# Attention on one Trainium2 core: V products of three or two key tiles right behind their scores, and PSUM banks named by hand

## The chip, the cores and the metric

The kernel runs on one core of one Trainium2 chip. The metric is device time in microseconds of one execution; lower is better. The time before is the median of three runs.

## The reference, cut to what matters

The reference is one transformer-like block on 2048 tokens of width 448, in float32. A modulation vector made from `c` scales and shifts two layer norms and gates two branches. The first branch is attention with 16 heads of width 28, the second a gated MLP whose gate mixes over the tokens. The change lies in attention:

```python
qkv = (x @ wqkv).reshape(B, S, 3, H, Dh).transpose(2, 0, 3, 1, 4)
q, k, v = qkv[0], qkv[1], qkv[2]
scores = jnp.einsum("bhqd,bhkd->bhqk", q, k) * (Dh ** -0.5)
p = softmax(scores, axis=-1)
o = jnp.einsum("bhqk,bhkd->bhqd", p, v)
attention = o.transpose(0, 2, 1, 3).reshape(B, S, D) @ wo
...
x = x + ga * attention
```

## The kernel before

The order of the work is written out by hand: each engine executes its instructions in the order in which the Python program issues them, and waits on semaphores where a buffer is not ready. Five engines take part: TensorE (PE) multiplies into PSUM banks, VectorE (DVE) and ScalarE (ACT) read PSUM, GpSimd (POOL) works in the on-chip memory only, and SyncE (SP) issues most transfers. PSUM has eight banks here; seven form the pool `ring`, from which `bank(name)` takes the next tile of 128 x 512 floats, and one is the pool `ps_o`, which holds a head's output sum `o_ps`. Which of the seven banks a tile of `ring` gets is decided by the pool while the program is built, and a tile's first matmul waits until the last reader of its bank is done.

After the norm of the input and the projections (`qk_unit`: a matrix of 128 x 512 in 11 matmuls into a bank `pq`, then two copies `qf` and `qh` by ScalarE and a subtraction by POOL), attention goes through 256 units `u`: 16 heads of 16 key tiles. For a unit

- `s_mm(u, qb)` multiplies one key tile of 128 keys with a quarter of the queries (512) into a bank `st_ps` (L603), and ScalarE takes the exponential into a tile `P` of the on-chip memory (L607). There are four quarters.
- `m_mm(j, kb)` makes, for the head that comes next, the scores of 128 queries with 512 keys into a bank `mt` (L572), and VectorE reduces them to a maximum per query (L577). This is needed since the exponential subtracts a maximum, which the transposed scores of `s_mm` carry as extra rows of the operand. `j` is 20 units ahead (`LEAD`).
- `pv_mm(u)` multiplies V with the four quarters of `P` and adds into `o_ps` (L618). V has 32 columns (28, and ones for the sum), so the four quarters use four column strips of 32 of the array. The profile shows two matmul records for each of these float32 matmuls, eight a unit.

The main loop before, for each unit `u`: four scores and four maximum scores in turn, then, on every even unit, the V products of units `u - 2` and `u - 1`. So TensorE changes 118 times into the V products and back in units 0 to 235. After these there is no next head, and the last 20 units have scores and V products only.

Around the units stand steps that are set to a slot, in two lists, `events` (issued before the unit's scores) and `late` (issued after its V products). At a head's end, `n_copy` has ScalarE copy `o_ps` out (L626), and `n_sum`, `n_recip`, `n_bcast`, `n_mul` and `n_scatter` divide it by its sum and store it by way of transfers, VectorE and POOL. Four units before a head, `m_max` reduces the maxima per query (L583, VectorE) and `m_fin` transposes them on TensorE (a bank `mtp`, L588), copies them twice on ScalarE (`nf`, `nh`), subtracts on POOL (`nl`), and stores two rows into the query operand by SP. Beside them run transfers and sums for a later stage (`ws_load`, `ws_add`, `ws_store`: SP and POOL).

Before unit 0 comes a ramp: 18 projection units with the first 81 maximum scores between their matmuls (`m_first`), from 86 to 152 us of the span.

Of the kernel before, what the change touches and what calls it, by code (L numbers as in the profile page):

```python
# [8 lines left out]
F32 = mybir.dt.float32  # L9
# [4 lines left out]
PSUM = bass.MemoryType.PSUM  # L14
DRAM = bass.MemoryType.DRAM

S, D, H, DH, FH = 2048, 448, 16, 28, 896
EPS = 1e-5
SCALE = DH ** -0.5
NT = S // 128  # L20
# [13 lines left out]
def tile_adaln_mha_gmlp(ctx, tc, x, wqkv, wo, w_in, w_spT, b_sp, w_out, cT, w_mod, out):  # L34
# [36 lines left out]
    class Halves:  # L71


        def __init__(self, n, lo, hi):
            self.n, self.views = n, (lo, hi)
# [34 lines left out]
    def ln_transpose(xns, full_pool, dsts, scol, bcol, engs, los=(pool,) * 4, mid=None, after=None):  # L110

        tps = []
        for c in range(4):
            tp = bank("tp")
            tps.append(tp)
            for t in range(4):
                pe.transpose(tp[:, t * 128 : (t + 1) * 128], xns[t][:, c * 128 : (c + 1) * 128], ident)  # L117
        if mid:
            mid()
        for c in (0, 2, 1, 3):  # L120
            tp = tps[c]
            f = full_pool.tile([128, 512], F32, name="hfull")
            if engs[c] is act:
                act.activation(f, tp, AF.Identity, scale=scol[:, c : c + 1], bias=bcol[:, c : c + 1])
            else:
                engs[c].tensor_scalar(
                    out=f, in0=tp, scalar1=scol[:, c : c + 1], scalar2=bcol[:, c : c + 1], op0=ALU.mult, op1=ALU.add
                )
            hi = dsts[:, c if c < 3 else 6, :]
            if engs[c] is act:  # L130
                act.activation(hi, f, AF.Copy)
            else:
                engs[c].tensor_copy(hi, f)
            if c < 3:
                sub(los[c], dsts[:, 3 + c, :], f, hi)
            else:
                sub(los[c], hi[64:128], f[64:128], hi[64:128])
            if after:
                after(c)


    ps = ctx.enter_context(ExitStack())
    ring = ps.enter_context(tc.tile_pool(name="ring", bufs=7, space=PSUM))
    ps_o = ps.enter_context(tc.tile_pool(name="ps_o", bufs=1, space=PSUM))

    att = ctx.enter_context(ExitStack())
    vpool = att.enter_context(tc.tile_pool(name="vpool", bufs=1))
# [13 lines left out]
    dve.memset(ones_r.bitcast(F32), 1.0)  # L161
    wms, xts, raws = {}, {}, {}

    def bank(name):
        return ring.tile([128, 512], F32, name=name, tag="s")

    def load_mod(pair, eng):
        for k in range(4):
# [48 lines left out]
    dve.tensor_tensor(out=silu, in0=cc_t, in1=ec, op=ALU.mult)  # L217

    pcs = {c: bank("pc") for c in (0, 2)}
    wu = bank("wu")  # L220

    def pe_fill(n, with_):
# [272 lines left out]
    for g in range(1, NG):  # L495
        if g == 3:
# [16 lines left out]
            def load_head(h, c0=0, c1=S):  # L513
                k, q = kst[h % 3], qst[h % 3]
                if h > 2:
                    sp.dma_start(q[84:86, :].bitcast(F32), q[86:88, :].bitcast(F32))
                for r0, i in ((0, 0), (56, 1), (28, 0)):
                    sp.dma_start(k[r0 : r0 + 28, c0:c1].bitcast(F32), qk_scr[i][D + h * DH : D + (h + 1) * DH, c0:c1])
                for r0, i in ((0, 0), (28, 1), (56, 0)):
                    sp.dma_start(q[r0 : r0 + 28, c0:c1].bitcast(F32), qk_scr[i][h * DH : (h + 1) * DH, c0:c1])  # L520
# [48 lines left out]
    def m_mm(j, kb):  # L569
        h, t = divmod(j, NT)  # L570
        mt = bank("mt")
        pe.matmul(  # L572
            mt, qst[h % 3][:, t * 128 : (t + 1) * 128], kst[h % 3][:, kb * 512 : (kb + 1) * 512], start=True, stop=True
        )
        if h not in pms:
            pms[h] = npool.tile([128, NT, 4], F32, name="pm")
        dve.tensor_reduce(out=pms[h][:, t, kb : kb + 1], in_=mt, axis=AX.X, op=ALU.max)  # L577
# [22 lines left out]
    def s_mm(u, qb):  # L600
        h, kt = divmod(u, NT)
        st = bank("st_ps")
        pe.matmul(st, kst[h % 3][:, kt * 128 : (kt + 1) * 128], qst[h % 3][:, qb * 512 : (qb + 1) * 512], start=True, stop=True)  # L603
        if qb % 2 == 0:
            ptiles[u, -1] = ppool.tile([128, 2, 512], F32, name="P")
        p = ptiles[u, -1][:, qb % 2, :]
        act.activation(p, st, AF.Exp, scale=SCALE)  # L607
        ptiles[u, qb] = p
# [4 lines left out]
    def pv_mm(u):  # L613
        h, kt = divmod(u, NT)
        if kt == 0:
            otile[h] = ps_o.tile([128, 512], F32, name="o_ps", tag="o")
        for qb in range(4):
            pe.matmul(  # L618
                otile[h][32 * qb : 32 * qb + 32, :], V[:, kt, h, :], ptiles.pop((u, qb)), start=kt == 0, stop=kt == NT - 1
            )  # L620
# [109 lines left out]
    LEAD = 20  # L730
    NU = H * NT
    events, late = {}, {}

    def at(slot, fn, *a, when=events):
        when.setdefault(slot, []).append((fn, a))

    for h in range(H):
        if h >= 2:
            at(h * NT - LEAD - 10, load_head, h)
        e0 = (h + 1) * NT  # L740
        at(e0 + 1, n_copy, h)
        at(e0 + 2, n_sum, h)
        at(e0 + 4, n_recip, h)
        at(e0 + 6, n_bcast, h)
        at(e0 + 8, n_mul, h)
        at(e0 + 9, n_scatter, h)
        at(h * NT + NT - LEAD, m_max, h)
        at(max(h * NT + NT - LEAD, -2), m_fin, h, when=late)
    for c, hl in ((0, 4), (1, 9), (2, 13)):
        for qb in range(4):  # L750
# [5 lines left out]
    for i in range(4):  # L756
        at(120 + 8 * i, wo_load, i)
        at(124 + 8 * i, wo_prep, i)
        at(200 + 8 * i, win_first, i)

    load_head(1)

# [15 lines left out]
    for i, (m, g) in enumerate(units):  # L778
        qk_unit((m,), g, {j: m_first for j in ((1, 3, 5, 7, 9) if i < 8 else (1, 4, 7, 10))})

    for u in range(NU + 1):
        for fn, a in events.pop(u, []):
            fn(*a)
        j = u + LEAD
        for qb in range(4 if u < NU else 0):
            s_mm(u, qb)
            if j < NU:
                m_mm(j, qb)
        if u % 2 == 0 and u > 0:
            pv_mm(u - 2)  # L790
            pv_mm(u - 1)
        for fn, a in late.pop(u, []):
            fn(*a)
    tail_events = {fn.__name__: [(fn, a)] for k in sorted(events) for fn, a in events[k]}

    def run_tail(*names):
        for nm in names:
            for fn, a in tail_events.pop(nm):
                fn(*a)

    run_tail("n_copy")


    att.close()
# [104 lines left out]
    h = H - 1  # L909
# [465 lines left out]
```

## Time and profile before

| | before |
|---|---|
| median of 3 runs | 1408.03 us (1407.81 to 1408.63) |
| profiled execution | 1407.25 us, its span 1405.5 us |
| granted TensorE clock | 1.0 |
| units 0 to 235 in the trace | 151.6 to 831.6 us |
| TensorE busy | 1393.3 us |
| VectorE busy | 1014.1 us |
| ScalarE busy | 788.9 us |

The profile shows for each group of instructions the engine, the tile written and the tiles read, the number, the busy time and the mean duration, and the idle time of the engine just before, with what ended it. Matmuls are pipelined, so one begins well before the last one's record ends: read their starts, not their durations. PEld are the weight loads, which overlap the matmuls; a load carries the wait for the bank of its matmul. Waits and chains are inferred from semaphore events.

### The profile page before, as it was taken

The page shows a single profiled execution, that of the slowest core. Times are in us where ns is not written, and L with a number is a line of the kernel's source. Part 1 is how long each engine was busy: PE and PEld are TensorE (multiplying, and loading weights), DVE is VectorE, ACT ScalarE, POOL GpSimd, SP SyncE. Part 2 cuts the span into 40 slices and gives each one's busy share as a digit, 9 for nine tenths or more (in the row PEclk, how much of TensorE's full clock was granted, in tenths as well). Part 3 has the DMA queues.
Part 4 walks back from the last instruction along what each step waited for, and adds up shares of the span by engine and source line. Part 5 has one row for each costly group of instructions (what it writes and reads, how often), then busy time and mean ns, then how long its engine had stood idle before and what let it go on. Part 6 is the DMA issues. An engine that isn't in the chain of part 4 may idle for free.

```text
span 1405.5 us, 20321 instructions
## 1 busy us (share of the span) xinstructions
PE 1393.3 (99%) x7164; PEld 981.2 (70%) x7164; DVE 1014.1 (72%) x1701; ACT 788.9 (56%) x1536; POOL 296.3 (21%) x284
## 2 busy tenths in 40 slices
PE   7999999999999999999999999999999999999999
PEld 7887655555555555555555554988998888888888
DVE  7798888888888888888888860751356655668574
ACT  4723677777777777777677779263234544434211
POOL 4234313122314243313200021100143430001000
PEclk9999999999999999999999999999999999999999
DMA  8564645555455556654422001534103333444453
GB/s 256 156 169 168 187 110 171 167 161 157 154 167 171 150 164 179 178 158 150 123 68 75 21 18 45 187 115 139 53 0 113 107 113 111 142 140 157 142 174 108
DMA packets 99377, 187.01 MB, mean 133 GB/s; under 512 B 17736, under 2 KB 29130, under 8 KB 96730
## 3 DMA queue, kind: packets, MB, share of 16 engines
q1 hardware_dynamic: 96846, 181.88, 43.0%
q10 hardware_dynamic: 2430, 3.84, 0.7%
q8 instruction: 56, 0.92, 0.3%
q14 instruction: 45, 0.37, 0.1%
HBM read 130.42 MB, written 50.46 MB: 129 GB/s over the span
## 4 chain that ended last, share of the span: by engine, by line
PE 96%; DMA 2%; DVE 1%; ACT 0%; issue 0%; SPq 0%; POOL 0%; DVEq 0%; ACTq 0%; POOLq 0%
PE st_ps L603 19%; PE o_ps L618 17%; PE mt L572 17%; PE acc L1143 6%; PE acc L1142 6%; PE acc L1144 6%; PE z_ps L1068 5%; PE z_ps L954 5%; PE pq L318 5%; PE wo_ps L824 3%; PE pv L300 2%; PE y_ps L1247 2%; PE y_ps L1248 2%; PE y_ps L1246 2%; PE tp L117 1%; DMA wm<-in_w_mod_dram 1%
## 5 line engine op out<-in xcount | busy, mean ns | idle before, releaser
L577 DVE TENSOR_REDUCE pm<-mt 128x1 f32<-128x512 f32 x1024 | 631.5, 682 | 110.0 <-PE mt L572 109.8
L607 ACT ACTIVATE P<-st_ps 128x512 f32<-128x512 f32 x1024 | 513.2, 621 | 150.0 <-PE st_ps L603 150.0
L603 PE MATMUL st_ps<-qst,kst 128*128 128x512 f32 x1024 | 407.5, 409 | 0.1
L572 PE MATMUL mt<-kst,qst 128*128 128x512 f32 x1024 | 402.1, 393 | 0.6 <-DVE pm L577 0.3
L603 PEld LDWEIGHTS st_ps<-qst,kst 128*128 128x128 f32 x1024 | 191.1, 187 | 151.4 <-issue 82.2
L618 PE MATMUL o_ps<-P,V 128*32 128x512 f32 x2048 | 247.5, 598 | 0.0
L572 PEld LDWEIGHTS mt<-kst,qst 128*128 128x128 f32 x1024 | 192.5, 188 | 32.9 <-DVE pm L577 2.3
L725 POOL TENSOR_TENSOR ws_raw<-ws_raw 128x512 f32<-128x512 f32 x80 | 102.9, 1287 | 282.8 <-DMA ws_raw<-in_w_spT_dram 270.4
L1030 ACT ACTIVATE wsp_h<-raw_sp 128x512 fp32r<-128x512 f32 x112 | 69.9, 631 | 154.4 <-PE acc L1144 103.6
L84 DVE TENSOR_TENSOR wsp_l<-raw_sp,wsp_h 128x512 fp32r<-128x512 f32 x112 | 82.0, 743 | 81.9 <-ACT wsp_h L1030 81.2
L618 PEld LDWEIGHTS o_ps<-P,V 128*32 128x32 f32 x2048 | 54.1, 109 | 123.5 <-issue 116.6
L1143 PE MATMUL acc<-wsp_l,heapA 128*128 128x512 f32 x224 | 87.4, 390 | 0.3 <-DVE wsp_l L84 0.2
L1142 PE MATMUL acc<-wsp_h,heapA 128*128 128x512 f32 x224 | 87.3, 390 | 0.0
L1144 PE MATMUL acc<-wsp_h,heapA 128*128 128x512 f32 x224 | 87.2, 389 | 0.0
L1143 PE MATMUL acc<-wsp_l,heapB 128*128 128x512 f32 x174 | 67.7, 389 | 0.0
L1144 PE MATMUL acc<-wsp_h,heapB 128*128 128x512 f32 x174 | 67.7, 389 | 0.0
L1142 PE MATMUL acc<-wsp_h,heapB 128*128 128x512 f32 x174 | 67.7, 389 | 0.0
L318 PE MATMUL pq<-heapD,heapD 128*128 128x512 f32 x196 | 61.9, 390 | 0.0
L1072 DVE BATCH_NORM_STATS2 stz<-z 128x6 f32<-128x448 f32 x32 | 19.9, 625 | 50.4 <-ACT z L1071 30.1
L1143 PEld LDWEIGHTS acc<-wsp_l,heapA 128*128 128x128 f32 x224 | 42.0, 188 | 9.6 <-DVE wsp_l L84 1.2
L1142 PEld LDWEIGHTS acc<-wsp_h,heapA 128*128 128x128 f32 x224 | 42.0, 188 | 9.0 <-DVE cD L1148 0.3
L1144 PEld LDWEIGHTS acc<-wsp_h,heapA 128*128 128x128 f32 x224 | 42.0, 188 | 8.8
(212 smaller groups left out, 1605.7 us busy)
## 6 DMA issues: line engine op xcount, KB each, us to landing
ws_raw<-in_w_spT_dram SPq DMA_DIRECT2D x160, 256.0 KB
ws_scr<-ws_raw SPq DMA_DIRECT2D x80, 256.0 KB
raw_sp<-ws_scr SPq DMA_DIRECT2D x80, 256.0 KB
kst<-qk_scr SPq DMA_DIRECT2D x45, 224.0 KB
qst<-qk_scr SPq DMA_DIRECT2D x45, 224.0 KB
raw_sp<-in_w_spT_dram SPq DMA_DIRECT2D x32, 256.0 KB
qk_scr<-qh SPq DMA_DIRECT2D x28, 256.0 KB
qk_scr<-ql SPq DMA_DIRECT2D x28, 256.0 KB
```

Of the source, the lines that this page charges most:

```text
L84: eng.tensor_tensor(out=dst, in0=a, in1=hi.bitcast(F32), op=ALU.subtract)
L318: pe.matmul(pq, wqk[:, b, m * 128 : (m + 1) * 128], hT[g][:, a, :], start=j == 0, stop=j == NST - 1)
L572: pe.matmul(mt, qst[h % 3][:, t * 128 : (t + 1) * 128], kst[h % 3][:, kb * 512 : (kb + 1) * 512], start=True, stop=True)
L577: dve.tensor_reduce(out=pms[h][:, t, kb : kb + 1], in_=mt, axis=AX.X, op=ALU.max)
L603: pe.matmul(st, kst[h % 3][:, kt * 128 : (kt + 1) * 128], qst[h % 3][:, qb * 512 : (qb + 1) * 512], start=True, stop=True)
L607: act.activation(p, st, AF.Exp, scale=SCALE)
L618: pe.matmul(otile[h][32 * qb : 32 * qb + 32, :], V[:, kt, h, :], ptiles.pop((u, qb)), start=kt == 0, stop=kt == NT - 1)
L725: pool.tensor_tensor(out=a, in0=a, in1=b, op=SUMS[i // 16][2])
L954: pe.matmul(ps_t, w1[:, b, f * 128 : (f + 1) * 128], h2T[g][:, a, :], start=j == 0, stop=j == NST - 1)
L1142: pe.matmul(acc[i], zh, hi, start=st == 0, stop=False)
L1143: pe.matmul(acc[i], zh, lo, start=False, stop=False)
L1144: pe.matmul(acc[i], zl, hi, start=False, stop=st == 7)
```

## The change

The order of units 0 to 235 becomes rounds of 3, 3, 3, 3, 2 and 2 key tiles for each head. A round issues all scores of its tiles with as many maximum scores between them, and then the V products of the same tiles, which before belonged to an earlier pair. The last 20 units keep their form. `n_copy` moves one unit earlier (before the first scores of the next head, since its V products now end with the head), and `m_max` moves from before a unit's scores to behind the V products, beside `m_fin`; both come after the round that holds the last maximum score of their head.

The seven banks are named in the program and no longer given out by the pool. In the ramp (`Ramp`) two banks go to the projections in turn and five to all else. In the units (`First`) a small count follows TensorE, VectorE and ScalarE in steps of a matmul, and gives each tile the bank that it holds to come free first. For this the pool `ring` is closed before the ramp, a second pool with seven named tiles stands in its place, and this one is closed again behind attention. `ps_o` is allocated before them.

```diff
     ps = ctx.enter_context(ExitStack())
-    ring = ps.enter_context(tc.tile_pool(name="ring", bufs=7, space=PSUM))
     ps_o = ps.enter_context(tc.tile_pool(name="ps_o", bufs=1, space=PSUM))
+    ring_s = ExitStack()
+    ring = [ring_s.enter_context(tc.tile_pool(name="ring", bufs=7, space=PSUM))]
...
+    chooser = [None]
+
     def bank(name):
-        return ring.tile([128, 512], F32, name=name, tag="s")
+        if chooser[0] is None:
+            return ring[0].tile([128, 512], F32, name=name, tag="s")
+        return ring[0].tile([128, 512], F32, name=name, tag=f"b{chooser[0](name)}", bufs=1)
...
-        at(e0 + 1, n_copy, h)
+        at(e0 if e0 < NU - LEAD else e0 + 1, n_copy, h)
...
-        at(h * NT + NT - LEAD, m_max, h)
+        at(h * NT + NT - LEAD, m_max, h, when=late if h else events)
...
+    class Ramp:
+        def __init__(self):
+            self.n = [0, 0]
+
+        def __call__(self, name):
+            k = int(name != "pq")
+            self.n[k] += 1
+            return 2 + self.n[1] % 5 if k else self.n[0] % 2
+
+    class First:
+        def __init__(self):
+            self.t, self.eng, self.free = 0.0, {}, [0.0] * 7
+
+        def __call__(self, name):
+            b = min(range(7), key=self.free.__getitem__)
+            self.t = max(self.t + 1, self.free[b] + 0.3)
+            a = max(self.eng.get(name, 0.0), self.t + 1.9)
+            self.eng[name] = a + (2.1 if name == "st_ps" else 2.6)
+            self.free[b] = a + (2.6 if name == "st_ps" else 3.0)
+            return b
+
+        def pause(self, n):
+            self.t += 3.75 * n + 1.5
+
+    ring_s.close()
+    ring[0] = ring_s.enter_context(tc.tile_pool(name="ring2", bufs=1, space=PSUM))
+    chooser[0] = Ramp()
+
     load_head(1)
...
-    for u in range(NU + 1):
-        for fn, a in events.pop(u, []):
+    chooser[0] = First()
+
+    def run_at(u, when):
+        for fn, a in when.pop(u, []):
             fn(*a)
-        j = u + LEAD
+
+    u = 0
+    for n in [n for _ in range(H) for n in (3, 3, 3, 3, 2, 2)]:
+        if u == NU - LEAD:
+            break
+        for k in range(u, u + n):
+            run_at(k, events)
+            for qb in range(4):
+                s_mm(k, qb)
+                m_mm(k + LEAD, qb)
+        for k in range(u, u + n):
+            pv_mm(k)
+        chooser[0].pause(n)
+        u += n
+        for k in range(u - n + 1, u + 1):
+            run_at(k, late)
+    for u in range(NU - LEAD, NU + 1):
+        run_at(u, events)
         for qb in range(4 if u < NU else 0):
             s_mm(u, qb)
-            if j < NU:
-                m_mm(j, qb)
-        if u % 2 == 0 and u > 0:
+        if u % 2 == 0 and u > NU - LEAD:
             pv_mm(u - 2)
             pv_mm(u - 1)
-        for fn, a in late.pop(u, []):
-            fn(*a)
+            chooser[0].pause(2)
+        run_at(u, late)
...
     run_tail("n_copy")
+    ring_s.close()
+    ring[0] = ps.enter_context(tc.tile_pool(name="ring", bufs=7, space=PSUM))
+    chooser[0] = None
```

## The prediction, made before the changed kernel ran

> **What bounds the kernel now.** I read the page first: the busy shares, the chain that ended last and the costliest groups.
>
> ```profile
> PE 1393.3 (99%) x7164; PEld 981.2 (70%) x7164; DVE 1014.1 (72%) x1701; ACT 788.9 (56%) x1536; POOL 296.3 (21%) x284
> ...
> PE st_ps L603 19%; PE o_ps L618 17%; PE mt L572 17%; PE acc L1143 6%; PE acc L1142 6%; PE acc L1144 6%; PE z_ps L1068 5%; PE z_ps L954 5%; PE pq L318 5%; PE wo_ps L824 3%; PE pv L300 2%; PE y_ps L1247 2%; PE y_ps L1248 2%; PE y_ps L1246 2%; PE tp L117 1%; DMA wm<-in_w_mod_dram 1%
> ...
> L577 DVE TENSOR_REDUCE pm<-mt 128x1 f32<-128x512 f32 x1024 | 631.5, 682 | 110.0 <-PE mt L572 109.8
> L607 ACT ACTIVATE P<-st_ps 128x512 f32<-128x512 f32 x1024 | 513.2, 621 | 150.0 <-PE st_ps L603 150.0
> ```
>
> Attention's three matmul lines (scores L603, maximum scores L572, V products L618) are 53% of the chain, all of it TensorE. VectorE's maxima and ScalarE's exponentials empty the banks and show idle time that ends on TensorE: the engine that sets the end is TensorE, for now. The next question is how much room the other two leave, which is seen inside one round. The timeline of one pair of key tiles, eight scores, eight maximum scores and then the V products of an earlier pair:
>
> ```profile
> 500.65 0.19 PEld L603 LDWEIGHTS st_ps<-qst,kst 128*128 128x128 f32 x1 [0.84 <-issue]
> 500.65 0.50 PE L603 MATMUL st_ps<-qst,kst 128*128 128x512 f32 x1
> 500.99 0.40 PE L572 MATMUL mt<-kst,qst 128*128 128x512 f32 x1
> ...
> 501.19 4.03 ACT L607 ACTIVATE P<-st_ps 128x512 f32<-128x512 f32 x8 [1.69 <-PE st_ps L603]
> 501.42 4.88 DVE L577 TENSOR_REDUCE pm<-mt 128x1 f32<-128x512 f32 x8 [0.85 <-PE mt L572]
> ...
> 504.20 0.39 PE L572 MATMUL mt<-kst,qst 128*128 128x512 f32 x1
> 504.52 0.16 PEld L618 LDWEIGHTS o_ps<-P,V 128*32 128x32 f32 x8 [0.36 <-issue]
> 504.98 0.13 PEld L618 LDWEIGHTS o_ps<-P,V 128*32 128x32 f32 x4 [0.30 <-issue]
> 505.41 0.13 PEld L618 LDWEIGHTS o_ps<-P,V 128*32 128x32 f32 x4 [0.30 <-issue]
> 506.38 0.50 PE L603 MATMUL st_ps<-qst,kst 128*128 128x512 f32 x1
> ```
>
> From start to start: the round takes 506.38 - 500.65 = 5.73 us. An ordinary matmul step is (504.20 - 500.99) / 14 = 0.229 us. The first step is 0.34 (its weights are loaded in the open: 0.11 more), the step into the V products 0.32, and these take 506.38 - 504.52 = 1.86 in four sets, 0.43 from set to set and more at the first and the last. Two sets are one key tile's products.
>
> ScalarE needs 4.03 us for eight exponentials; with the group's 0.62 for one, they end (4.03 - 0.62) / 7 = 0.487 apart. VectorE needs 4.88 for eight maxima, with 0.68 for one: 0.60 apart. A score and a maximum score together take TensorE only 0.459. So inside the burst of scores both readers fall behind, and they catch up during the V products. That is the fact on which the forecast rests.
>
> **The long stretch: fewer changes of kind.** The change does 60 rounds of three tiles and 28 of two over units 0 to 235, where there were 118 rounds of two. In the built kernels' instruction order every matmul is there as before; only the places differ. A round of three is a round of two plus eight steps and two sets: 5.73 + 8 x 0.229 + 2 x 0.43 = 8.42. So 118 x 5.73 = 676.1 becomes 60 x 8.42 + 28 x 5.73 = 665.6: **-10.5 us** if nothing waits. The stretch itself is known:
>
> ```profile
> 151.60:831.60 680.00, 679.92 (x3775) 387.35 (x3774) 579.23 (x971) 488.13 (x987) 156.25 (x140) 1.00 0.48 138
> ```
>
> 680.0 against 676.1: all transposes and waits of today are 3.9 us, most of them at the transposes, which stay. I take 0.7 of them as gone.
>
> **The long stretch: the banks run out in a round of three.** Seven banks hold scores and maximum scores. When may a matmul follow a reader? A wait in the present kernel shows it:
>
> ```profile
> 242.92 3.67 DVE L577 TENSOR_REDUCE pm<-mt 128x1 f32<-128x512 f32 x6
> 244.04 0.40 PE L572 MATMUL mt<-kst,qst 128*128 128x512 f32 x1
> 244.25 0.19 PEld L603 LDWEIGHTS st_ps<-qst,kst 128*128 128x128 f32 x1 [0.26 <-DVE pm L577]
> 244.60 0.40 PE L572 MATMUL mt<-kst,qst 128*128 128x512 f32 x1
> ```
>
> The second of these maxima ends at 242.92 + 0.68 + 0.60 = 244.20; the weight load that waited for it starts 0.05 later, at 244.25. It normally starts with the matmul before (244.04). From 244.04 to 244.60 are 0.56 where two steps are 0.46: so a load that is 0.21 late costs 0.10, and 0.11 of lateness is free. A bank must thus be read empty 0.05 before the load's latest time, which is the nominal start of its matmul less 0.23 plus 0.11.
>
> Times from the round's start, by the pair above: maximum score k (from 0) starts at 0.34 + 0.459k; exponential k ends at 0.54 + 0.62 + 0.487k = 1.16 + 0.487k; maximum k ends at 0.77 + 0.68 + 0.60k = 1.45 + 0.60k.
> - In a pair the tightest is the last matmul, maximum score 7 at 3.55, load by 3.43, banks read by 3.38. Fifteen tiles stand before it, at most six may be held, so nine must be read: five exponentials (the fifth ends at 3.11) and four maxima (3.25). Just enough; the trace has hardly a wait.
> - In a three, maximum score 10 would start at 4.93, banks read by 4.76. Of 21 tiles 15 must be read: eight exponentials (4.57) and six maxima (4.45) make 14. The next end at 5.05 and 5.06: 0.29 late. The following score finds its bank. Maximum score 11 would now start at 5.68, with 17 to be read by 5.51: nine exponentials and seven maxima are 16, the next ends at 5.54: 0.03 late.
>
> So each round of three waits about 0.32 us however well the banks are chosen, and 60 x 0.32 = **+19.2**. In the fifteen rounds of three that open a head, the copy of the last head's output (L626) stands before the exponentials; today it delays them so:
>
> ```profile
> 200.56 0.50 PE L603 MATMUL st_ps<-qst,kst 128*128 128x512 f32 x1
> 200.75 0.60 ACT L626 ACTIVATE osb<-o_ps 128x512 f32<-128x512 f32 x1 [1.47 <-PE o_ps L618]
> 201.25 3.04 ACT L607 ACTIVATE P<-st_ps 128x512 f32<-128x512 f32 x6
> ```
>
> First exponential at 0.69 where it was 0.54. With exponentials 0.15 later the last wait above grows from 0.03 to 0.14: 15 x 0.11 = **+1.6**. The copy's move by one unit changes nothing more.
>
> The Trainium skill, page "TensorEngine Tiling (Array Packing)", section "PSUM Bottleneck", warns that tiling speeds up TensorE but not the emptying of PSUM. Read on a round's mean, twelve maxima at 0.60 are 7.2 of 8.42 us, it would not bite and the sum would keep the whole -10.5; read on the burst, as the rows above have it, it does.
>
> **What else moves, at nothing.** The V products now follow their own scores. In a three, exponential 11 ends at 6.52 and the third tile's products start not before 5.38 + 0.32 + 1.72 = 7.42; in a pair exponential 7 ends at 4.57 and the second tile's products start at 3.87 + 0.86 = 4.73. If that cover fails in the fifteen pairs after a transpose, where ScalarE starts some 0.3 later, it is 15 x 0.2 = 3 at most. The head's maximum (L583), its transpose, two small ScalarE copies, the subtraction on POOL and two transfers on SP's queue come one unit earlier against the scores; the maximum stands on VectorE behind twelve maxima, that end at 8.05 + 0.3 and so just before the V products do (8.4 + 0.3). In the built order SP's and VectorE's queues hold the same instructions in the same order as before, and on POOL only the subtraction passes a preparation of wo, in two heads. The transfers have two rounds of two, 11 us, until the next head's scores.
>
> **The ramp before (86 to 152 us).** Two edges and a gain.
>
> ```profile
> 86.42 0.19 PEld L318 LDWEIGHTS pq<-heapD,heapD 128*128 128x128 f32 x1
> 86.62 0.40 PE L318 MATMUL pq<-heapD,heapD 128*128 128x512 f32 x1
> 87.36 0.60 DVE L256 COPY bc_gb<-pc 128x448 f32<-128x448 f32 x1
> ...
> 115.69 0.40 PE L318 MATMUL pq<-heapD,heapD 128*128 128x512 f32 x1
> 116.18 0.50 PE L572 MATMUL mt<-kst,qst 128*128 128x512 f32 x1
> 116.52 0.63 PE L318 MATMUL pq<-heapD,heapD 128*128 128x512 f32 x2
> ...
> 120.24 0.40 PE L318 MATMUL pq<-heapD,heapD 128*128 128x512 f32 x1
> 121.28 0.39 PE L318 MATMUL pq<-heapD,heapD 128*128 128x512 f32 x1
> ...
> 151.61 0.39 PE L603 MATMUL st_ps<-qst,kst 128*128 128x512 f32 x1
> 151.87 0.60 ACT L324 ACTIVATE qf<-pq 128x512 f32<-128x512 f32 x1 [2.14 <-PE pq L318]
> ```
>
> The old pool closes before the ramp, and in the built order the first pq matmul then waits for that copy of bc_gb, which ends at 87.96: load at 88.01, 1.5 us later than now (everything on TensorE is queued behind it). The first score waits for the last qf (its named bank was a pq bank): 152.47 + 0.05 + 0.11 against 151.61, +1.0. In return maximum scores in the ramp wait for the reduce five tiles back, not for the last one. From 120.24 over the next maximum score to 121.28 two steps take 1.04 instead of 0.46: 0.58 saved; from 115.69 to 116.52 they take 0.83, 0.37 saved, and two more like this one follow before 119: -1.7 in all. The sum is **+0.8**; both edges could be hidden or doubled, so -1.7 to +3.
>
> **The sum.** -10.5 - 0.7 + 19.2 + 1.6 + 0.8 = +10.4. The 0.32 leans on 0.487: with 0.477 exponential 8 ends at 4.98 and is the fifteenth read, so the waits are 0.22 and 0.01, some -5 over the 60 rounds; with 0.497 exponential 9 ends at 5.63 and they are 0.29 and 0.12, some +5. I take +9.5, a little under, since the first wait of a round leaves VectorE time that I have not credited. From the profiled execution's 1407.25 us this gives 1416.8; the median of the runs stands 0.8 above it, so I say 1417.5 for the median.
>
> **The rivals.**
> - *Faster: banks come free earlier than I count.* The break-even is a wait of (10.5 - 0.8) / 60 = 0.16 us in a round, half of mine. For it: the present kernel shows hardly a wait, and a pair is at the edge by my count as well, so a systematic 0.1 us would pass unseen there. Against: the rates 0.487 and 0.60 are measured on eight in a row. With no wait at all: 1408.0 - 10.5 - 0.7 + 0.8 = 1397.6; with a third of it, 1404. Chance 0.18.
> - *Nothing to measure: gain and waits even out* at 0.16: 1408. Chance 0.06.
> - *The names do not act:* that the pool gives the banks out as before. The built order speaks against it, since the waits are on other tiles than before; the price would be more waits, 1420 and above. Chance 0.05, in "slower".
> - *The clock falls.* The page shows a granted clock of 1.00 through this stretch (the window above), with the short waits that it has. If pauses of 0.3 us in each round brought it down to a half in one round of three in ten, that is 6 x 8.42 = 51 us: 1459. The Trainium skill, page "TensorE: Matmul & The Clock Gate", section "A second HAM failure mode: psum-queue depth-cycling", tells of such pauses between groups of matmuls as PSUM banks cycle. Chance 0.01.
>
> **How the numbers follow.** My case, slower by the bank waits, has 0.70, and with the two other slow ones 0.76; faster 0.18, same 0.06, with 0.2% (2.8 us) as what a measurement of this kernel can tell. My case alone would span 1412 to 1422 (the bounds on 0.487, the ramp and the 3 us of the pairs, which won't all fall together). That holds under 8 in 10, so the range reaches down over "same" to a third of the waits: 1405 to 1422.
>
> **What the profile after would show.** The steps are right if there are about 30 fewer pauses of 0.84 us before L603's weight loads after V products, and if the other weight loads of L603 and those of L572 show new idle time released by VectorE and ScalarE, near maximum score 10 of each three, 15 to 20 us longer in sum; a head (16 tiles) taking 46.6 to 46.9 us against 46.2 (680.0 x 16 / 236 = 46.1). If a head takes 45.4 the bank count is wrong; if the third tile's V products wait for ScalarE, the cover that I named is gone; if the first pq doesn't start about 1.5 us later, the edge of the pool is.

## The result, and the profile after

The changed kernel takes 1418.49 us (median of 6 runs, 1417.81 to 1419.47) against 1407.91 of the kernel before on the same chip: ratio 1.007, interval 1.0059 to 1.008. It is 10.6 us slower; 9.5 was forecast (1417.5 for 1408.03). The profiled execution spans 1417.6 us, 12.1 more than that of before.

The lines of the page after that answer to those of before: TensorE's busy time has grown by 11 us with the same number of instructions, and the two readers' has not.

```profile
PE 1404.5 (99%) x7164; PEld 980.8 (69%) x7164; DVE 1011.4 (71%) x1701; ACT 785.2 (55%) x1536; POOL 294.1 (21%) x284
...
L583 DVE TENSOR_REDUCE pm<-mt 128x1 f32<-128x512 f32 x1024 | 627.8, 682 | 124.3 <-PE mt L578 124.2
L613 ACT ACTIVATE P<-st_ps 128x512 f32<-128x512 f32 x1024 | 509.5, 648 | 150.0 <-PE st_ps L609 149.8
```

By the chain and the busy shares nothing seems to have happened: TensorE is 98% of the chain now. What TensorE's time is made of shows in the waits of its weight loads. First the kernel before, then after, both in units 0 to 235 (us in total, times, longest):

```profile
PEld st_ps L603 <- issue: 74.6, 89, 0.8
PEld st_ps L603 <- DVE pm L577: 15.2, 28, 0.8
PEld st_ps L603 <- ACT P L607: 11.8, 54, 0.5
...
PEld mt L572 <- ACT P L607: 0.7, 3, 0.3
```

```profile
PEld st_ps L609 <- DVE pm L583: 36.9, 44, 0.8
PEld mt L578 <- ACT P L613: 29.9, 123, 0.3
PEld st_ps L609 <- ACT P L613: 29.8, 153, 0.3
PEld st_ps L609 <- issue: 23.5, 28, 0.8
...
PEld mt L578 <- DVE pm L583: 3.2, 14, 0.2
```

The loads of maximum scores hardly waited for ScalarE (3 times), and now do 123 times; those of scores do 153 times, not 54. (The "longest 0.8" are the pauses behind V products, put down to a reader that had long been done; they are fewer, as there are fewer rounds. A wait counted here includes up to 0.11 us that is free, and idle time that loads always have.) The timeline of one round of three, from its first score to the next round's, shows where:

```profile
396.80 0.50 PE L609 MATMUL st_ps<-qst,kst 128*128 128x512 f32 x1
...
397.39 5.99 ACT L613 ACTIVATE P<-st_ps 128x512 f32<-128x512 f32 x12 [2.81 <-PE st_ps L609]
...
399.96 0.24 DVE L640 RECIPROCAL rt<-rt 128x16 f32<-128x16 f32 x1
...
400.57 0.41 PE L609 MATMUL st_ps<-qst,kst 128*128 128x512 f32 x1
400.80 0.19 PEld L578 LDWEIGHTS mt<-kst,qst 128*128 128x128 f32 x1
400.82 0.48 PE L578 MATMUL mt<-kst,qst 128*128 128x512 f32 x1
400.98 0.19 PEld L609 LDWEIGHTS st_ps<-qst,kst 128*128 128x128 f32 x1
401.14 0.40 PE L609 MATMUL st_ps<-qst,kst 128*128 128x512 f32 x1
401.39 0.19 PEld L578 LDWEIGHTS mt<-kst,qst 128*128 128x128 f32 x1 [0.23 <-DVE pm L583]
401.39 0.50 PE L578 MATMUL mt<-kst,qst 128*128 128x512 f32 x1
401.50 0.19 PEld L609 LDWEIGHTS st_ps<-qst,kst 128*128 128x128 f32 x1
401.73 0.40 PE L609 MATMUL st_ps<-qst,kst 128*128 128x512 f32 x1
401.96 0.19 PEld L578 LDWEIGHTS mt<-kst,qst 128*128 128x128 f32 x1 [0.27 <-ACT P L613]
401.97 0.49 PE L578 MATMUL mt<-kst,qst 128*128 128x512 f32 x1
...
402.30 0.40 PE L609 MATMUL st_ps<-qst,kst 128*128 128x512 f32 x1
...
402.87 2.78 PE L624 MATMUL o_ps<-P,V 128*32 128x512 f32 x24
...
405.58 0.49 PE L609 MATMUL st_ps<-qst,kst 128*128 128x512 f32 x1
```

After the first, the steps are 0.23 to 0.24 up to 400.57. Then the loads of three maximum scores in a row (8, 9 and 10, counted from 0) come late, the second for VectorE, the third for ScalarE; the first is too short a wait to be marked. From score to score, where two steps are 0.46, 400.57 to 401.14 takes 0.57, 401.14 to 401.73 takes 0.59 and 401.73 to 402.30 takes 0.57: each late load costs 0.11 to 0.13. The round takes 405.58 - 396.80 = 8.78 us against 8.42 without waits. The twelve exponentials run on from 397.39 to 403.38 without a pause, and the V products (from 402.87) don't wait for them. (This second round of a head also holds VectorE's reciprocal of the last head's sum, at 399.96, in the midst of the maxima. In the third and fourth rounds, which have none, the long steps lie around maximum scores 9 and 10; they take as long, 8.79 and 8.83 us.)

Over units 0 to 235:

```profile
153.20:846.50 693.30, 693.27 (x3792) 385.95 (x3792) 577.32 (x973) 484.46 (x987) 154.18 (x138) 1.00 0.47 135
```

693.3 against 680.0, at the same granted clock of 1.00. The last twenty units give 0.9 back (their last score comes 38.35 after unit 236's first, against 39.28): before, the V products of units 234 and 235 still stand in that stretch, after the change they stand ahead of it.

### The profile page after: what moved, and what is told of

The parts are those of the page before. It is cut to its first block, busy times and chain, and to the rows that moved or that the text cites. A ratio compares the mean times of both kernels' runs of the same rounds, so it can differ in the third digit from the quotient of the medians.

```text
span 1417.6 us, 20287 instructions
## 1 busy us (share of the span) xinstructions
PE 1404.5 (99%) x7164; PEld 980.8 (69%) x7164; DVE 1011.4 (71%) x1701; ACT 785.2 (55%) x1536; POOL 294.1 (21%) x284
## 4 chain that ended last, share of the span: by engine, by line
PE 98%; DMA 1%; DVE 1%; SPq 0%; issue 0%; ACT 0%; DVEq 0%; ACTq 0%
PE st_ps L609 18%; PE mt L578 18%; PE o_ps L624 17%; PE acc L1203 6%; PE acc L1205 6%; PE acc L1204 6%; PE z_ps L1129 5%; PE pq L324 5%; PE z_ps L1015 5%; PE wo_ps L885 3%; PE pv L306 2%; PE y_ps L1308 2%; PE y_ps L1309 2%; PE y_ps L1307 2%; PE tp L117 1%; DMA wm<-in_w_mod_dram 1%
## 5 line engine op out<-in xcount | busy, mean ns | idle before, releaser
L578 PE MATMUL mt<-kst,qst 128*128 128x512 f32 x1024 | 415.4, 406 | 0.0
L624 PE MATMUL o_ps<-P,V 128*32 128x512 f32 x2048 | 241.4, 597 | 0.0
L624 PEld LDWEIGHTS o_ps<-P,V 128*32 128x32 f32 x2048 | 60.1, 109 | 120.3 <-issue 109.8
```

Source lines behind the costliest of these rows:

```text
L578: pe.matmul(mt, qst[h % 3][:, t * 128 : (t + 1) * 128], kst[h % 3][:, kb * 512 : (kb + 1) * 512], start=True, stop=True)
L624: pe.matmul(otile[h][32 * qb : 32 * qb + 32, :], V[:, kt, h, :], ptiles.pop((u, qb)), start=kt == 0, stop=kt == NT - 1)
```

## The experiments

The question: is it the banks that cost the time in rounds of three, or the V products being right behind their own scores, or the naming of the banks?

Each ratio is against runs of the kernel before on the same chip (median 1406.14 us on one, 1408.09 on the other).

**Banks that come free earlier, in threes and in pairs.** Two runs with the same edit, one in each kernel; the first has its count adapted too. They leave half of the keys out of the maximum, so they serve for the time alone.

```diff
-        dve.tensor_reduce(out=pms[h][:, t, kb : kb + 1], in_=mt, axis=AX.X, op=ALU.max)
+        dve.tensor_reduce(out=pms[h][:, t, kb : kb + 1], in_=mt[:, 0:256], axis=AX.X, op=ALU.max)
...
-        act.activation(p, st, AF.Exp, scale=SCALE)
+        act.activation(p, st, AF.Exp, scale=SCALE * 0.1)
```

> The changed kernel, but VectorE's maximum reads only 256 of the 512 columns (the maximum over half the keys; the exponent is scaled by a tenth so that nothing overflows), so that a bank of maximum scores comes free about 0.3 us earlier and maxima end about 0.33 apart instead of 0.60; the count that names the banks is told so (its 2.6 and 3.0 for a maximum score become 1.45 and 1.9). TensorE's work is untouched. My theory (in rounds of three the seven banks run out, 0.3 to 0.4 us a round): the waits go, and what is left is the gain of fewer changes of kind: units 0 to 235 at 45.3 us a head instead of 47.0, 1394 to 1397 in all, and 8 to 11 us under the same edit in the kernel before. Rival (the V products right behind their own scores cost it, by waiting for the last exponentials or in the changes of kind themselves): ScalarE is untouched, so the loss stays, 9 us or more over the same edit in the kernel before, some 1413.

> The kernel before with the same edit (maximum over 256 of 512 columns, exponent scaled by a tenth), as the base of comparison. My theory: pairs wait little on banks, so little changes: 1403 to 1407, a head at 45.9 to 46.1 us. Rival: the same, since it says nothing of this kernel.

Threes: 1392.34 us, ratio to the kernel before 0.9903 (0.9888 to 0.9917). Pairs: 1401.42, 0.9966 (0.9955 to 0.9976). The expectation gave 1394 to 1397 and 1403 to 1407: both come out about 1.6 us under that, about as far as the kernel before does on this chip (1406.14, where the other runs have 1407.9), and the 9.1 between them lie in the 8 to 11 expected. Units 0 to 235 of the threes and then of the pairs:

```profile
152.70:818.40 665.70, 665.65 (x3792) 402.13 (x3792) 404.99 (x973) 484.74 (x987) 154.67 (x138) 1.00 0.48 141
```

```profile
150.00:826.40 676.40, 676.40 (x3775) 393.56 (x3774) 402.02 (x972) 487.65 (x987) 156.32 (x140) 1.00 0.48 139
```

The threes are 10.7 us shorter than the pairs here, and a round of three takes 8.39 to 8.43 us, where the sum without waits had 8.42. The two windows don't hold quite the same work: at unit 236's first score the pairs still lack the V products of two tiles. Up to the last score, where both have issued the same matmuls, 715.68 becomes 703.97: -11.7, where the sum gave -10.5 and -0.7. The waits of the loads in this run of threes:

```profile
PEld o_ps L624 <- issue: 102.6, 327, 0.4
PEld st_ps L609 <- issue: 60.4, 72, 0.8
PEld o_ps L624 <- ACT P L613: 15.4, 57, 0.3
PEld mtp L594 <- issue: 12.6, 15, 0.8
PEld st_ps L609 <- ACT qf L330: 1.2, 1, 1.2
```

No load of a score waits for a reader in the loop any more. The V products now do show 57 waits on the exponentials, but of 0.3 at most, where the normal idle time before such a load is the same 0.3, and those of a round of three take 2.71 us to the next round's first score (median), as they do with full maxima. So the gain from fewer changes of kind is real, and the time of the maxima takes it away: with full maxima these rounds cost 693.3 - 665.7 = 27.6 us more, the pairs only 3.6.

**One bank less, in threes.**

```diff
-            b = min(range(7), key=self.free.__getitem__)
+            b = min(range(6), key=self.free.__getitem__)
```

> The changed kernel with one bank taken away: First chooses among six of its seven banks. My theory: the two readers together empty a bank each 0.487 x 0.60 / (0.487 + 0.60) = 0.27 us, so with one bank less every round of three waits about that much more, and the pairs, which were just enough, start to wait as well by about the same: 88 rounds x 0.27 to 0.32 = 24 to 28 us over the changed kernel, a head at 48.6 to 48.9. Rival (the loss is not one of banks): within 5 us of the changed kernel.

1443.18 us, 1.0245 (1.0231 to 1.0259): about 25 us over the changed kernel (the ratios 1.0245 and 1.007 differ by 0.0175, of 1408). A round of three takes 9.07 to 9.17, 0.2 to 0.4 more, the two pairs of a head 6.14 and 5.92, 0.25 and 0.16 more, and a head 48.5 us, just under the 48.6 to 48.9 expected. In sum the dose does what the rates of the readers said; the pairs have a little less of it.

**Order and names apart.** One kernel has the rounds, with the pool's banks; the other has the names, with the old order.

```diff
-    ring_s.close()
-    ring[0] = ring_s.enter_context(tc.tile_pool(name="ring2", bufs=1, space=PSUM))
-    chooser[0] = Ramp()
...
-    chooser[0] = First()
```

> The changed kernel's order with rounds of three and two, but all banks given out by the pool as before (no Ramp, no First, no second pool). My theory: the waits of a round of three stay and grow, since the pool names a bank without the count: 18 us over the kernel before, some 1426, with a head at 47.3 us; the ramp as before (first score at 151.6 us). Rival (the names cost the time and the order gains): at or under 1408.

1428.61 us, 1.0168 (1.015 to 1.0185): 22 to 24 us over the kernel before, a head 47.7 us. The rounds alone lose more than the change does; the names give about half of it back. In units 0 to 235, where nothing but the choice of banks differs, it is 704.2 us against 693.3 with the names.

```diff
     for u in range(NU + 1):
         for fn, a in events.pop(u, []):
             fn(*a)
         j = u + LEAD
...
         if u % 2 == 0 and u > 0:
             pv_mm(u - 2)
             pv_mm(u - 1)
+            chooser[0].pause(2)
```

(These lines are against the kernel before; the second pool, `Ramp` and `First` are as in the change.)

> The kernel before in its order (pairs, V products of the earlier pair, n_copy and m_max where they were), with the banks named by Ramp and First, the second pool and all. My theory: the loop is as before or 1 us shorter (a head at 46.1), the ramp costs 0.8 (first pq matmul 1.5 us later, the waits in the middle of the ramp gone, first score 1.0 later): 1407 to 1409. Rival (the names cost the time): near the changed kernel, 1415 or more.

1405.48 us against 1406.14, 0.9998 (0.9989 to 1.0008): no difference. In pairs the names neither cost nor give anything that the total can tell, a head 46.0 us. The trace splits it: units 0 to 235 take 678.35 us instead of 680.00, most of it in the last pair of a head (5.74 instead of 5.83), while from the first matmul of `pc` ahead of the ramp to the first score it is 66.6 instead of 65.8.

**V products right behind, in pairs.**

```diff
-    for n in [n for _ in range(H) for n in (3, 3, 3, 3, 2, 2)]:
+    for n in [n for _ in range(H) for n in (2, 2, 2, 2, 2, 2, 2, 2)]:
```

> The changed kernel with rounds of two tiles only (eight a head): V products still right behind their own scores, names as in the changed kernel. My theory: it is the third tile that costs, by the bank waits, not that the V products follow their own scores; so a head falls from 47.0 to 46.2 to 46.4 us, with a wait of 0.2 at each of the transposes, whose maximum now comes right behind eight maxima: 1407 to 1411. Rival (right behind costs it): the loss stays, 1415 or more.

1410.65 us, 1.0019 (1.001 to 1.0028): 2.7 over the kernel before, where threes have 10.6. A head takes 46.4: ordinary pairs 5.73, the pair before the transpose 5.99, the one after it 5.90. So it is the third tile that costs. Being right behind, with the later `m_max`, costs 0.2 at each transpose (5.99, against 5.77 with the names in the old order), whose maximum then stands behind eight maxima; the pair after it took 5.90 in the old order too. In threes the round before a transpose takes 8.83 against 8.79 without one, so this cost is not among theirs.

**Two attempts at a better kernel.** Three edits in the old order with names (the third is one argument of First, `[6.0] + [0.0] * 6` for the free times), and the same in rounds counted in quarter tiles.

```diff
-        act.activation(nh, nf, AF.Copy)
+        pool.tensor_copy(nh, nf)
...
             v_tile(4 * g + 2 + k)
+            if g == 3 and k == 0:
+                mod_col("cb", 2, 0, 1.0)
+                mod_bc("gb", 2, 1)
+                pads(2, pool)
...
-    mod_col("cb", 2, 0, 1.0)
-    mod_bc("gb", 2, 1)
```

> An attempt at a better kernel: the kernel before in its order, with Ramp and First, and three edits. The second small copy at a transpose (nh) goes from ScalarE to POOL, so that the exponentials behind it start 0.3 us earlier and the wait of 0.16 to 0.2 us in the pair behind each of 15 transposes goes: -2.5 to -3.3. The copy of bc_gb is issued before the last V projection and the memsets of the third operand pair after it, so that the first pq matmul waits for the last V copy only: 0.6 instead of 1.5. First is told that the bank of the last pq is late, so that the first score doesn't wait 1.0. In all 4 to 5 us under the names alone, 5 under the kernel before: a head at 45.8 to 45.9. Rival (the waits at the transposes hide something else that is late): no change against the names alone.

1403.63 us against 1408.09, 0.9965 (0.9952 to 0.9979): faster than both kernels. The pair behind a transpose takes 5.71 to 5.73 where the names alone have 5.90, as expected; but the head stays at 46.0, where 45.8 to 45.9 was expected, and units 0 to 235 gain only 0.4 us against the names alone (677.98, 678.35). The ramp's first pq matmul does wait for the V copy only:

```profile
87.50 0.50 PE L324 MATMUL pq<-heapD,heapD 128*128 128x512 f32 x1 [0.63 <-ACT V L310]
```

What of the 4.5 us is whose isn't settled. Of the loop's gain the trace shows where it went: 14 pairs behind a transpose give 2.6 us, but the loop's first round takes 8.75 us where it took 7.88 with the names alone, and most other rounds 0.01 to 0.02 more. The two profiles span 1402.1 (names alone) and 1401.8; they are from two chips, on which the kernel before differs by 1.9 us, and don't show all of the difference that the ratios give.

> The same three edits in the changed kernel, with rounds counted in quarter tiles: 9, 9, 9, 9, 12, 8 and 8 score pairs a head, V products right behind of the tiles that are complete. My theory: nine fit the banks, so one change of kind a head is saved (0.33) and only the round of twelve waits (0.3); against the pairs with the same edits nothing or up to 1 us is gained: a head at 45.8 to 46.0, 3 to 6 us under the kernel before. Rival (any round over eight costs): 2 us or more over the pairs with the same edits.

1406.40 us, 0.9985 (0.9976 to 0.9994), some 2.8 over the pairs with the same edits (up to the last score 719.72 against 717.26): my expectation was missed, and the rival's price of 2 or more was met. Not by its reason, though: rounds of nine score pairs (a score and a maximum score each) do fit the banks (6.19 to 6.22 us where two tiles' V products follow, 5.73 and two steps of 0.23). But the first of a head, behind the copy of the last head's output, takes 6.32, and the round of twelve 8.83, 0.41 over 8.42; that eats the 0.33 of the change of kind saved.

## Why the prediction was right, point by point

- *Fewer changes of kind, -10.5, and 0.7 of old waits.* Right: -11.7 between the two kernels with short maxima, up to the last score. It is hidden in the changed kernel and had to be uncovered. One count was off without harm: 117 changes into the V products and back, not 118, end before unit 236's first score, and the last twenty units hold one more, which the change saves as well. So the transposes and waits of before were nearer 6 us in this stretch than 3.9; the number of changes saved is 30 all the same.
- *Bank waits, +19.2 and +1.6.* Right in kind and place, too small in size. An ordinary round of three takes 8.79 and the one that opens a head 8.90, so the waits are 0.37 and 0.48, where 0.32 and 0.43 were forecast. What the reckoning lacked stands in the timeline: the first exponential starts at 397.39 - 396.80 = 0.59 in the round, not 0.54 as in the pair before. In the built order that exponential is held by one more semaphore instruction on ScalarE, for the tile of `P` that it overwrites; the trace has it (here at 397.33) in 59 of the 60 rounds of three, and in none of the rounds whose first exponential starts at 0.54. A start 0.05 later moves every exponential, and in the prediction's own count it turns the 0.03 at maximum score 11 into 0.08, which makes 0.37; that this makes the wait longer was reckoned and not tested. For the rounds that open a head it explains nothing, since there VectorE ends that last wait: their 0.05 stays open.
- *Where the count was off.* It passed over maximum score 9: it would start at 4.47, banks read by 4.30, with 13 of 19 tiles to be read, and the thirteenth (maximum 5) ends at 4.45, 0.15 late; maximum score 10 then adds 0.14, and the sum is 0.32 as before. The trace has it so: in the fifteen third rounds of a head the steps around maximum scores 9, 10 and 11 are 0.12, 0.20 and 0.03 longer than usual (medians).
- *What the waits cost in all.* Up to the last score the time grew by 12.3 us (719.28 to 731.62), where the terms said 9.6. With the short maxima it falls by 11.7, so the waits are 24.0, where +19.2 and +1.6 were forecast.
- *The ramp, +0.8.* Right by its parts: the first pq matmul waits for the copy of bc_gb, the first score for the last qf.

```profile
88.18 0.60 DVE L262 COPY bc_gb<-pc 128x448 f32<-128x448 f32 x1
...
88.92 0.47 PE L324 MATMUL pq<-heapD,heapD 128*128 128x512 f32 x1 [1.33 <-DVE bc_gb L262]
...
152.58 0.60 ACT L330 ACTIVATE qf<-pq 128x512 f32<-128x512 f32 x1 [2.13 <-PE pq L324]
...
153.23 0.50 PE L609 MATMUL st_ps<-qst,kst 128*128 128x512 f32 x1 [0.75 <-ACT qf L330]
```

  The pq matmul starts 2.3 later than before, of which 0.8 is older than the change (the first of the four matmuls for `pc` just ahead of it is at 86.61 and was at 85.80); the first score 1.6 later, 0.8 without that.
- *What was costed at nothing* stayed so: the V products don't wait for their exponentials, and the transposes not beyond their pause.
- *The total* came nearer than its terms, and that is luck in part: attention up to the last score is 2.7 over them, and taking +9.5 for their sum of +10.4 went the wrong way, while in the profiles 1.9 us come back behind attention (from the last score to the end 532.7, was 534.6) that no edit touches; the other kernels' profiles have 532.3 to 533.7 there, so I count it as no effect of the change.
- *The signs it named.* The pauses of 0.84 us before loads of scores are 30 fewer (103, now 73), as said, and the first pq starts 1.5 later. A head takes 47.0 us, just over the 46.6 to 46.9. The other waits of these loads for VectorE and ScalarE grew by 47 us (15.9 to 63.0), not by 15 to 20: the sign took them for the time lost, but the time lost is the 24 above, since part of each such wait is free.
- *The rivals.* "Faster, banks come free earlier" fell, since every round of three waits; its price without waits, 1397.6 (10.4 under the kernel before), was nearly what the threes with short maxima show against the pairs with them (9.1 under). "The names do not act" fell with the rounds on the pool's banks, 10.9 us slower in units 0 to 235 than with names. The granted clock stayed at 1.00 in spite of waits of 0.1 to 0.3 us in every round of three. What the Trainium skill, page "TensorE: Matmul & The Clock Gate", section "A second HAM failure mode: psum-queue depth-cycling", tells of, a clock that falls and rises as TensorE idles briefly between groups of matmuls, did not happen here. What the Trainium skill, page "TensorEngine Tiling (Array Packing)", section "PSUM Bottleneck", warns of, that emptying PSUM may become the limit, held in the burst, though of matmuls on the whole array (128 x 128), and though VectorE is busy only 577 of 693 us.

## What to carry to other kernels

Where readers empty banks more slowly than TensorE fills them, the mean shares of the engines say nothing on how long a burst may be: count the tiles issued against those read at each matmul, with the banks as the limit. Count at each of them, and not only at the one that looks tightest. Here, with exponentials 0.49 and maxima 0.60 us apart and 0.23 us for a matmul, eight score pairs a burst just fit seven banks, nine fit too away from a head's first round, and rounds of twelve cost more than the changes of kind that they save. To see whether a gain is there and hidden, shorten the suspected reader in both kernels and compare these two.

## What the runs showed that was not expected

That rounds of three on the pool's own banks lose 22 us, twice what the same rounds lose with the new names, was more than the 18 forecast: which bank a tile gets matters in rounds of three, whose readers fall behind (10.9 us in units 0 to 235), and hardly in pairs (1.7 us there, 0.9998 in all).
